# Attention and two feed-forward layers on one core: GpSimd's normalising in two multiplications, coefficients later, a plan that looks ahead

## The chip, the core and the metric

The kernel runs on one core of a Trainium2 chip. The core has five engines that run side by side, each through its own list of instructions in order: TensorE (PE in the tables, with its weight loads as PEld), VectorE (DVE), ScalarE (ACT), GpSimd (POOL) and SyncE (SP), which here only issues transfers. They meet at semaphores. The metric is the device time of one execution in microseconds, the median of the runs shown; less is better.

## What is computed

Two batches of 12 heads, 448 tokens, head dimension 64, causal attention in float32; its output, laid out as 896 tokens by 768, goes through two feed-forward layers of 768 by 2048 by 768. The first has the gate `h * clip(h+3, 0, 6) / 6`, the second a rational function of `h` with six coefficients `a` and `b`:

```
attn = softmax(mask(q @ k.T / 8)) @ v          # per head; x = attn as (896, 768)
h = x @ w_in;  x = (h * clip(h + 3, 0, 6) / 6) @ w_out
h = x @ w_in2
P = a[0] + a[1]*h + a[2]*h**2 + a[3]*h**3
Q = 1 + |b[0]|*|h| + |b[1]|*h**2
out = (P / (Q + 1e-6)) @ w_out2
```

The weights arrive as float64; the kernel takes their two halves apart and builds from each a rounded float32 part and a rest, and every product of the feed-forward layers is the sum of three products (high by high, high by rest, rest by high).

## The kernel before, and what sets its order

**Attention** works on 12 pairs of heads, numbered 0 to 11. Queries are cut into seven pieces of 64, and piece `r` (0 to 6) sees 64(r+1) keys; two heads lie side by side on the 128 partitions. For each pair:

- SP loads keys, queries and values (`kr`, `qr`, `v`; L401, L406, L407).
- PE multiplies the scores into four PSUM banks (L434, 28 products).
- VectorE adds the mask, takes each row's maximum and copies the piece to SBUF as `e<r><x>`, where x is the pair's parity (L446). So there are two sets of `e` buffers, and pair n+2 can enter them only when pair n has left.
- ScalarE takes the exponential in place and sums it (L453, an activation and a read of its accumulator).
- The sums get 1e-9 added (L463 on ScalarE or L465 on VectorE) and are inverted on VectorE (L469), in two parts: pieces 6, 5, 0 first, then 4, 3, 2, 1. This is in `stat`.
- The pieces are normalised, that is multiplied by the inverse, on ScalarE (L475), VectorE or GpSimd (both L477). Before the change GpSimd does the three widest pieces, r = 6, 5 and 4, of the pairs 1 to 9, and the others do the rest.
- PE transposes the normalised pieces in four groups of four (L483), VectorE or ScalarE moves each group to SBUF as `et` (L335, L333), and PE multiplies by the values (L503). ScalarE and VectorE split the result into `xh` and `xl`.

**The products** (L722) start when the attention of most pairs is done: 128 chunks of three weight tiles, 2304 products of 128 by 128 by 448, of which 18 belong to a chunk. For each chunk ScalarE and VectorE build the weights out of the raw bits: `full` (L617), `tail` (L623), shift and sign (L627, L633), the high part `w` (L333) and the rest (L651). A ring of four `w` buffers lets them run ahead of PE. Every third product chunk from the second layer on is prepared early, stored to DRAM (`kept`) and fetched later. The coefficients `ca` and `cb` (L593, L594) are needed only by the rational function in the second half; VectorE makes `cneg` of them (L597) and ScalarE `cabs` (L600).

**The order** is not written by hand. `add` gives each operation a kind, a time at which it is wanted, the engines it can run on with a price for each, and what it reads and writes. `order` then plays a list scheduler: at each step it takes, of all operations whose inputs are planned, the one that can begin first, and of several with the same beginning the one that is due first (`DUE` by kind, added to its wanted time). `STAY` is a handicap for a change of PE's tiling. The chosen order is what each engine's list of instructions gets; on the chip only the order counts, not the planned times.

Of the kernel before, what the change touches and what calls it, by code (L numbers as in the profile page):

```python
# [35 lines left out]
class Program:  # L36
# [15 lines left out]

    TILING = {"scores": "quarters", "apply": "columns"}
    DRAIN = 0.16
    STAY = 2.84

    def __init__(self, rings, banks, due):
        self.rings, self.banks, self.due = rings, banks, due
# [2 lines left out]
    def add(self, kind, at, engines, fn, *args, reads=(), writes=(), new=()):  # L61

        self.ops.append((kind, at, engines, fn, args, tuple(reads), tuple(writes), tuple(new)))

    def order(self):
# [42 lines left out]
        due = [op[1] + self.due[op[0]] for op in ops]  # L110
        result, tiling = [], ""
        while can:
            best = None
            for n, t in can.items():
                room, want = 0.0, {}
                for tag, key in ops[n][7]:
                    want[tag] = want.get(tag, 0) + 1
                    if tag == "w" and key != queue[-1]:
                        room = 1e9
                for tag, k in want.items():  # L120
                    if tag in self.rings:
                        keys, size = rings[tag], self.rings[tag]
                        for back in range(size - k + 1, size + 1):
                            if len(keys) >= back:
                                room = max(room, released.get(keys[-back], 1e9))
                    else:
                        times = sorted(x for x in banks if x is not None)
                        if live[tag] + k > self.banks[tag] or len(times) < k:
                            room = 1e9
                        else:  # L130
                            room = max(room, times[k - 1])
                if room >= 1e9:
                    continue
                turn = "pe" in t and self.TILING.get(ops[n][0], "") != tiling
                for e, cost in ops[n][2].items():
                    mine = max(t[e], free[e], room), due[n] + self.STAY * turn, n, e, cost
                    if best is None or mine < best:
                        best = mine
            if best is None:
                raise RuntimeError("no room")  # L140
            begin, _, n, e, cost = best
            if e == "pe" and self.TILING.get(ops[n][0], "") != tiling:
                tiling = self.TILING.get(ops[n][0], "")
                begin = max(begin, free[e] + self.DRAIN)
            start[n], end[n], where[n] = begin, begin + cost, e
            free[e] = end[n]
            del can[n]
            got = []
            for tag, key in ops[n][7]:
                if tag == "w":  # L150
                    queue.pop()
                if tag in self.rings:
                    rings[tag].append(key)
                else:
                    b = min((x, b) for b, x in enumerate(banks) if x is not None)[1]
                    banks[b] = None
                    held[key] = tag, b
                    live[tag] += 1
                    got.append(b)
            given[n] = got  # L160
            for key in {*ops[n][5], *ops[n][6]}:
                touch[key] -= 1
                last[key] = max(last.get(key, 0.0), end[n] + self.DELAY[e]["dve"])
                if not touch[key]:
                    released[key] = last[key]
                    if key in held:
                        tag, b = held.pop(key)
                        banks[b] = last[key]
                        live[tag] -= 1
            for u in users[n]:  # L170
                missing[u] -= 1
                if not missing[u]:
                    can[u] = earliest(u)
            result.append((begin, len(result), n))
# [9 lines left out]
def c_act(n):  # L184
    return 0.051 + n / 1200
# [8 lines left out]


def c_norm(n, r, w):
    fast = {"dve": 0.07 + w / 960, "act": 0.06 + w / 1200}
    if 0 < n < 10 and r > 3:
        return {"pool": 0.25 + w * 0.00252}
    return fast if n == 0 or r > 3 else {**fast, "pool": 0.25 + w * 0.00252}  # L200


def c_pe(n, passes):
# [7 lines left out]
def c_mm(n, passes):  # L211
# [2 lines left out]


DUE = {
    "load": -66.8,
    "keep": 0.0,
    "fetch": -20.0,
    "load v": -6.2,  # L220
    "norm": -71.7,
    "scores": 73.4,
    "max": -32.0,
    "exp": 10.8,
    "bias": 4.9,
    "reciprocal": -29.8,
    "transpose": -21.5,
    "move": 6.5,
    "apply": 23.1,
    "x hi": 5.2,  # L230
    "x rest": 62.2,
    "constants": -8.8,
    "w load": -87.2,
    "magnitude": 45.8,
    "tail": -50.0,
    "shift": -31.3,
    "sign": -2.7,
    "w hi": 63.9,
    "w rest": -7.0,
    "product": 0.0,  # L240
    "relu": 8.8,
    "gate": 1.1,
    "g hi": -5.5,
    "g rest": 21.7,
    "y hi": 20.8,
    "y rest": 12.6,
    "affine": 7.8,
    "times": -0.9,
    "abs": 6.2,
    "times2": -4.8,  # L250
    "slope": -0.4,
    "square": -3.2,
    "ln": 21.9,
    "exp2": -3.5,
    "over": 16.5,
    "newton": 17.1,
    "value": -6.1,
    "r hi": 19.2,
    "r rest": 3.2,
    "out": -3.6,  # L260
    "store": 7.5,
}
PAIR = 5.6

# [19 lines left out]
def tile_attention_moe_moe2(  # L284
# [36 lines left out]
        "p": 4, "qy": 3,  # L321
    }
    rings.update({f"e{r}": EB for r in range(NCH)})
    prog = Program(rings, {"s": 4, "t": 2, "o": 2, "sum": 8}, DUE)
    add = prog.add
    bank = [psum.tile([P, 512], F32, name=f"bank{n}") for n in range(prog.BANKS)]

# [143 lines left out]
    def a_norm(e, n, r):  # L471
        t, at_ = es[n % EB][r][:, :(r + 1) * CP], LINEUP.index(r)
        by = tiles["stat", n][:, 2, at_:at_ + 1]
        if e is nc.scalar:
            e.activation(t, t, AF.Copy, scale=by)  # L475
        else:
            e.tensor_scalar(t, t, by, None, ALU.mult)  # L477

    def a_transpose(e, n, g, banks):
        pt = tiles["pt", n, g] = bank[banks[0]]  # L480
# [39 lines left out]
    for n in range(len(pairs)):  # L520
# [59 lines left out]
                new=[("o", ("o", n))] if a == 0 else (),  # L580
            )
        b, hp = pairs[n]
        add("x hi", t, {"act": c_act(S) + 0.04}, a_hi, n, reads=[("o", n)], writes=[("x", hp, b)])
        add("x rest", t, {"dve": c_dve(S)}, a_lo, n, reads=[("o", n)], writes=[("x", hp, b)])


# [11 lines left out]

    def c_abs(e):
        e.activation(cabs, cb, AF.Abs)  # L600

    add("constants", 20, {"dma": 0.1}, c_load, writes=["c"])
    add("constants", 30, {"dve": 0.1}, c_neg, reads=["c"], writes=["cneg"])
    add("constants", 30, {"act": 0.1}, c_abs, reads=["c"], writes=["cabs"])


    raw, full, tail, split = {}, {}, {}, {}
# [57 lines left out]
    def add_chunk(i, t, early=()):  # L665
# [12 lines left out]
        add("shift", t, dve, w_shift, i, reads=[("tail", i)], writes=[("full", i)])  # L678
        add("sign", t, dve, w_sign, i, reads=[("raw", i)], writes=[("full", i)])
        x = [("x", hp, b) for hp in range(KM) for b in range(B)] if early and i == early[0] else []  # L680
        add(
            "w hi", t, act, w_hi, i, bool(early), reads=[("full", i)] + x, writes=[key],
            new=[(tag, key)],
# [194 lines left out]
    for n, c in enumerate(early):  # L878
        add_chunk(c, base + 40 + (whole - 45) * n / len(early), early)
    while i < len(chunks):  # L880

        side = chunks[i][0][0] == 2
        n = 1 if not side else 2 if chunks[i + 2][0][0] == 2 else 3
# [72 lines left out]
```

## Time and profile before

| | us |
|---|---|
| median of 3 runs | 552.57 (552.07 to 553.94) |
| the profiled execution, whole | 552.57 |
| its span, first to last instruction | 550.8 |
| PE busy in the span | 537.6 (98%) |
| VectorE, ScalarE, GpSimd busy | 429.5, 404.0, 39.6 |

The profiled execution has the median's time, and 1.77 us of it lie outside the span. The span falls into two stages. Up to about 95 us the core does attention, with the first 48 products mixed in; from there to 547.3 us PE runs products, and 3.5 us of copy and store close it. A busy engine need not be the bound in a stage: what tells is who waited for whom. In the rows, times count from the start of the span; an entry in square brackets is the idle time of an engine just before the row and what ended it. On PE a busy time includes waiting that falls within a run of merged instructions, so the time from one row's start to the next row's start is the better measure.

### The profile page before, as it was taken

How to read it: one execution, taken by the hardware profiler on the slowest of the kernel's cores; microseconds unless marked ns; L12 is line 12 of the kernel's file. 1: busy time of each engine (PE TensorE's matmuls, PEld its weight loads, DVE VectorE, ACT ScalarE, POOL GpSimd, SP SyncE). 2: the span in 40 equal slices, each digit the busy share in tenths (PEclk: the TensorE clock that was granted, in tenths of full speed). 3: DMA queues.
4: the chain of work that ended last, by engine and by line, in shares of the span. 5: the costliest groups of instructions: out<-in, count | busy, mean ns of one | idle time of the engine just before them, and what ended most of it. 6: DMA issues, size and time to landing. Idle time of an engine off the chain costs nothing.

```text
span 550.8 us, 9402 instructions
## 1 busy us (share of the span) xinstructions
PE 537.6 (98%) x3236; PEld 491.7 (89%) x3236; DVE 429.5 (78%) x953; ACT 404.0 (73%) x907; POOL 39.6 (7%) x51
## 2 busy tenths in 40 slices
PE   6889999999999999999999999999999999999997
PEld 5667788999999999999999999999999999999996
DVE  3769896799999997877776279999899988975420
ACT  4989997888888987767676269877787678755410
POOL 2555531000000000000000000000000000000000
PEclk9899999999999999999999999999999999999999
DMA  5764224267777878677776431154234324236100
GB/s 168 217 190 136 64 65 137 68 225 249 229 251 237 270 229 295 224 265 249 249 245 202 135 115 58 59 174 141 87 115 125 105 87 134 96 114 200 50 35 33
DMA packets 39312, 87.13 MB, mean 158 GB/s; under 512 B 4704, under 2 KB 14688, under 8 KB 39264
## 3 DMA queue, kind: packets, MB, share of 16 engines
q1 hardware_dynamic: 39104, 86.30, 49.1%
q8 instruction: 25, 0.41, 0.3%
q10 hardware_dynamic: 160, 0.23, 0.2%
q14 instruction: 23, 0.19, 0.1%
HBM read 71.18 MB, written 15.34 MB: 157 GB/s over the span
## 4 chain that ended last, share of the span: by engine, by line
PE 90%; ACT 6%; SPq 1%; DMA 1%; issue 1%; POOL 1%; DVE 0%; POOLq 0%; ACTq 0%
PE bank L722 84%; ACT e L453 3%; PE bank L503 2%; PE bank L483 2%; PE bank L434 2%; DMA cb<-in_b 1%; PE bank L383 1%; ACT e L475 1%; ACT et L333 1%; POOL e L477 0%; SPq L401 0%; ACT xh L333 0%; SPq L407 0%; SPq L406 0%; ACT full L617 0%
## 5 line engine op out<-in xcount | busy, mean ns | idle before, releaser
L722 PE MATMUL bank<-yh,w 128*128 128x448 f32 x384 | 112.1, 362 | 0.0
L722 PE MATMUL bank<-rh,w 128*128 128x448 f32 x384 | 97.2, 362 | 0.0
L722 PE MATMUL bank<-xh,w 128*128 128x448 f32 x384 | 94.0, 364 | 0.0
L722 PE MATMUL bank<-ph,w 128*128 128x448 f32 x384 | 92.6, 362 | 0.0
L651 DVE TENSOR_TENSOR w<-full,w 128x384 fp32r<-128x384 f32 x96 | 53.1, 555 | 47.2 <-ACT w L333 47.0
L333 ACT ACTIVATE w<-full 128x384 fp32r<-128x384 f32 x96 | 50.4, 528 | 53.2 <-PE bank L722 52.7
L623 ACT ACTIVATE tail<-raw 128x384 uint32<-128x384 uint8 x128 | 69.7, 557 | 20.9 <-DVE full L627 18.1
L617 ACT ACTIVATE full<-raw 128x384 f32<-128x384 f32 x128 | 68.9, 554 | 15.9 <-DVE w L651 15.0
L627 DVE SCALAR_TENSOR_TENSOR full<-full,tail 128x384 uint32<-128x384 uint32 x128 | 69.6, 555 | 12.7 <-ACT full L617 11.3
L722 PEld LDWEIGHTS bank<-rh,w 128*128 128x128 f32 x384 | 71.7, 187 | 5.6 <-DMA w<-kept 0.6
L722 PEld LDWEIGHTS bank<-ph,w 128*128 128x128 f32 x384 | 72.0, 188 | 4.9
L722 PEld LDWEIGHTS bank<-xh,w 128*128 128x128 f32 x384 | 71.6, 188 | 5.3 <-DVE stat L469 0.4
L722 PEld LDWEIGHTS bank<-yh,w 128*128 128x128 f32 x384 | 72.0, 187 | 4.7
L633 DVE SCALAR_TENSOR_TENSOR full<-raw,full 128x384 uint32<-128x384 uint32 x128 | 69.0, 554 | 1.6
L722 PE MATMUL bank<-yl,w 128*128 128x448 f32 x192 | 69.5, 362 | 0.0
L722 PE MATMUL bank<-rl,w 128*128 128x448 f32 x192 | 54.6, 362 | 0.0
L722 PE MATMUL bank<-xl,w 128*128 128x448 f32 x192 | 53.9, 362 | 0.0
L722 PE MATMUL bank<-pl,w 128*128 128x448 f32 x192 | 53.9, 362 | 0.0
L453 ACT ACTIVATE e<-e,stat 128x192 f32<-128x192 f32 (+6 forms) x84 | 42.4, 522 | 6.6 <-DVE stat L446 6.6
L477 POOL TENSOR_SCALAR e<-e,stat 128x448 f32<-128x448 f32 (+4 forms) x31 | 36.9, 1201 | 47.1 <-DVE stat L469 42.3
L446 DVE CUSTOM_DVE_ANT_0 e<-bank,mask 128x192 f32<-128x192 f32 (+6 forms) x84 | 31.8, 415 | 8.8 <-PE bank L434 8.6
L722 PEld LDWEIGHTS bank<-yl,w 128*128 128x128 f32 x192 | 36.0, 188 | 2.5
(58 smaller groups left out, 739.2 us busy)
## 6 DMA issues: line engine op xcount, KB each, us to landing
raw<-in_w SPq DMA_DIRECT2D x128, 384.0 KB, 3.6
kept<-ws SPq DMA_DIRECT2D x32, 384.0 KB, 4.2
w<-kept SPq DMA_DIRECT2D x32, 384.0 KB, 3.4
kr<-in_kT SPq DMA_DIRECT2D x24, 112.0 KB, 2.8
out_T<-o SPq DMA_DIRECT2D x12, 224.0 KB, 2.8
qr<-in_qT SPq DMA_DIRECT2D x22, 112.0 KB, 3.1
v<-in_v SPq DMA_DIRECT2D x12, 128.0 KB, 3.1
v<-in_v SPq DMA_DIRECT2D x12, 96.0 KB, 2.8
```

The lines of the kernel that those rows point to most:

```text
L333: e.activation(out, in_, AF.Copy)
L434: e.matmul(tiles["sc", n, r][halves[slot]], q[halves[j], r * CP:w], k[halves[j], :w], start=True, stop=True,)
L446: e.tensor_tensor_reduce(es[n % EB][r][:, :w], tiles.pop(("sc", n, r)), mask[:, S - w:], -0.125, 3.0e38, ALU.add, ALU.min, tiles["stat", n ...
L453: e.activation(t, t, AF.Exp, bias=stat[:, 0, at_:at_ + 1], scale=-1.0, accum_out=stat[:, 1, at_:at_ + 1],)
L477: e.tensor_scalar(t, t, by, None, ALU.mult)
L483: e.transpose(to[:, x], es[n % EB][r][:, c * P:(c + 1) * P], ident)
L617: e.activation(full[i], high, AF.Copy, scale=TO_F32)
L623: e.activation(tail[i], top, AF.Copy, bias=-31.0 / 64.0, scale=1.0 / 32.0)
L627: e.scalar_tensor_tensor(bits, bits, 3, tail.pop(i), ALU.logical_shift_left, ALU.bitwise_or)
L633: e.scalar_tensor_tensor(bits, raw.pop(i)[:, :, :, 1], 0x80000000, bits, ALU.bitwise_and, ALU.bitwise_or)
L651: e.tensor_tensor(split[i][:, 1], full.pop(i), split[i][:, 0], ALU.subtract)
L722: e.matmul(sums[which, m, b], split[i][:, w, j, :], x, start=k == 0 and n == 0, stop=last and n == 2,)
```

## The change

Five things are changed together.

1. Normalising on VectorE and GpSimd becomes one `tensor_scalar` with two multiplications, by the inverse and then by 1.0, in place of one multiplication and no second operation. The result is the same.
2. All seven pieces of the pairs 1 to 9 are now normalised on GpSimd; only pairs 0, 10 and 11 have a choice of engines.
3. For the first four weight chunks the high part and the rest may be done on GpSimd too; the plan puts the high parts of chunks 0 to 3 there and the rests of chunks 0 and 2.
4. The coefficients are loaded among the products (after chunk 8's weights in the plan) and `cneg` and `cabs` made later still.
5. The planner looks ahead: up to 90 us of planned time, an operation that begins up to `LOOK` later than the earliest one on its engine counts as beginning equally early, and the one that is due first is taken. The due times of most kinds, `STAY`, the price of `x hi` and the number of banks for the values' product (2 to 1) change with it.

```diff
-    STAY = 2.84
+    STAY = 3.13
+    LOOK = {"pe": 0.153, "dve": 0.041, "act": 0.000, "pool": 1.171, "dma": 0.000}
+    UNTIL = 90.0
...
-                    mine = max(t[e], free[e], room), due[n] + self.STAY * turn, n, e, cost
-                    if best is None or mine < best:
-                        best = mine
+                    at = max(t[e], free[e], room)
+                    begins[e] = min(begins.get(e, at), at)
+                    found.append((at, due[n] + self.STAY * turn, n, e, cost))
...
+            begin, _, _, n, e, cost = min(
+                (max(at, begins[e] + self.LOOK[e] * (at < self.UNTIL)), late, at, n, e, cost)
+                for at, late, n, e, cost in found
+            )
...
 def c_norm(n, r, w):
-    fast = {"dve": 0.07 + w / 960, "act": 0.06 + w / 1200}
-    if 0 < n < 10 and r > 3:
-        return {"pool": 0.25 + w * 0.00252}
-    return fast if n == 0 or r > 3 else {**fast, "pool": 0.25 + w * 0.00252}
+    fast = {"dve": 0.13 + w / 1920, "act": 0.185 + w / 1200}
+    slow = {"pool": 0.12 + w * 0.0012}
+    return {**fast, **slow} if n == 0 or n > 9 else slow
...
-    "norm": -71.7,
-    "scores": 73.4,
+    "norm": -208.80,
+    "scores": 150.38,
...
-    prog = Program(rings, {"s": 4, "t": 2, "o": 2, "sum": 8}, DUE)
+    prog = Program(rings, {"s": 4, "t": 2, "o": 1, "sum": 8}, DUE)
...
-            e.tensor_scalar(t, t, by, None, ALU.mult)
+            e.tensor_scalar(t, t, by, 1.0, ALU.mult, ALU.mult)
...
-    add("constants", 20, {"dma": 0.1}, c_load, writes=["c"])
-    add("constants", 30, {"dve": 0.1}, c_neg, reads=["c"], writes=["cneg"])
-    add("constants", 30, {"act": 0.1}, c_abs, reads=["c"], writes=["cabs"])
...
+        act, dve = ({**e, "pool": c} if i < 4 else e for e, c in ((act, 0.5), (dve, 1.05)))
...
+        if i == 16:
+            add("constants", t, {"dma": 1.2}, c_load, reads=[("w", 8)], writes=["c"])
+        if i == 24:
+            add("constants", t, {"dve": 0.1}, c_neg, reads=["c", ("w", 20)], writes=["cneg"])
+            add("constants", t, {"act": 0.1}, c_abs, reads=["c", ("w", 20)], writes=["cabs"])
```

The tables say little by themselves; what follows is what the engines' lists show. The names are buffers: `e61` is piece 6 in the set of the odd pairs, `stat1` the statistics of pair 1, `et0_1` the second transposed group of pair 0, `bank2` a PSUM bank, `full0` the weights of chunk 0.

GpSimd, from the first normalising on (pairs 1 and 2), before:

```order
L477 TENSOR_SCALAR e61_104<-e61_104,stat1_214 128x448
L477 TENSOR_SCALAR e51_103<-e51_103,stat1_214 128x384
L477 TENSOR_SCALAR e41_102<-e41_102,stat1_214 128x320
L477 TENSOR_SCALAR e60_97<-e60_97,stat2_281 128x448
L477 TENSOR_SCALAR e50_96<-e50_96,stat2_281 128x384
```

and the same place in the changed kernel, where pair 1 has all seven pieces:

```order
L484 TENSOR_SCALAR e61_104<-e61_104,stat1_211 128x448
L484 TENSOR_SCALAR e51_103<-e51_103,stat1_211 128x384
L484 TENSOR_SCALAR e01_98<-e01_98,stat1_211 128x64
L484 TENSOR_SCALAR e41_102<-e41_102,stat1_211 128x320
L484 TENSOR_SCALAR e31_101<-e31_101,stat1_211 128x256
L484 TENSOR_SCALAR e21_100<-e21_100,stat1_211 128x192
L484 TENSOR_SCALAR e11_99<-e11_99,stat1_211 128x128
```

All seven pieces of a pair stand in a row where three stood, the part with the pieces 6, 5 and 0 first. Further on, between pairs 5 and 6, GpSimd's list in the changed kernel has the first weight chunk:

```order
L484 TENSOR_SCALAR e21_100<-e21_100,stat5_559 128x192
L484 TENSOR_SCALAR e11_99<-e11_99,stat5_559 128x128
L342 CAST w0_714<-full0_463 128x384
L654 TENSOR_TENSOR w0_714<-full0_463,w0_714 128x384
L484 TENSOR_SCALAR e60_97<-e60_97,stat6_656 128x448
```

The high part (CAST) and the rest (TENSOR_TENSOR) of chunk 0 have come to stand between two pairs; before, GpSimd had no weight work.

VectorE, around the first inverse of pair 1 (`stat1`, the RECIPROCAL of 3 columns; ISA is the mask and maximum of a piece), before:

```order
L335 COPY et0_2_291<-bank6_79 128x512
L446 ISA e00_91,stat2_281<-bank2_75,mask_90 128x64
L446 ISA stat2_281 128x1
L469 RECIPROCAL stat1_214<-stat1_214 128x3
L446 ISA e40_95,stat2_281<-bank4_77,mask_90 128x320
```

and in the changed kernel:

```order
L472 TENSOR_SCALAR stat1_211<-stat1_211 128x3
L453 ISA e00_91,stat2_281<-bank2_75,mask_90 128x64
L453 ISA stat2_281 128x1
L476 RECIPROCAL stat1_211<-stat1_211 128x3
L453 ISA e50_96,stat2_281<-bank5_78,mask_90 128x384
```

The copy of pair 0's third transposed group has gone from ahead of this inverse to a place behind it.

ScalarE, around the coefficients (`cabs`) in the middle of pair 4's exponentials, before:

```order
L453 ACTIVATE e20_93,stat4_455<-e20_93,stat4_455 128x192
L453 ACTIVATE e30_94,stat4_455<-e30_94,stat4_455 128x256
L600 ACTIVATE cabs_111<-cb_109 128x2
L453 ACTIVATE e10_92,stat4_455<-e10_92,stat4_455 128x128
L617 ACTIVATE full0_563<-raw0_250 128x384
L453 ACTIVATE e61_104,stat5_561<-e61_104,stat5_561 128x448
L475 ACTIVATE e30_94<-e30_94,stat4_455 128x256
L475 ACTIVATE e10_92<-e10_92,stat4_455 128x128
```

and in the changed kernel:

```order
L460 ACTIVATE e20_93,stat4_461<-e20_93,stat4_461 128x192
L340 ACTIVATE xh1_84<-bank2_75 128x448
L460 ACTIVATE e50_96,stat4_461<-e50_96,stat4_461 128x384
L460 ACTIVATE e30_94,stat4_461<-e30_94,stat4_461 128x256
L460 ACTIVATE e10_92,stat4_461<-e10_92,stat4_461 128x128
L620 ACTIVATE full1_541<-raw1_274 128x384
L620 ACTIVATE full2_551<-raw2_291 128x384
L340 ACTIVATE et3_1_557<-bank5_78 128x512
L626 ACTIVATE tail0_565<-raw0_223 128x384
```

The coefficients and the normalising are gone from there, and weight work has come in.

## Rows read from the trace of the kernel before

**Rows 1.** Chain of work that ended last: start, us, engine, what, line, instructions.

```profile
8.56 3.16 ACT e L453 x12
...
42.42 0.48 ACT et L333
...
64.09 0.45 ACT tail L623
...
68.81 1.67 PE bank L434 x22
70.48 1.91 PE bank L503 x32
...
86.72 1.90 PE bank L483 x16
...
95.35 451.96 PE bank L722 x2256
```

**Rows 2.** Windows: stretch, us, busy PE, PEld, DVE, ACT, POOL, granted clock, DMA.

```profile
5.98:41.89 35.91, 29.19 (x356) 21.73 (x357) 26.14 (x122) 29.68 (x108) 14.84 (x12) 0.95 0.69 198
41.89:66.83 24.94, 23.34 (x294) 18.51 (x293) 21.55 (x84) 24.94 (x85) 15.05 (x12) 1.00 0.36 100
```

**Rows 3.** Timeline of PE: start, us, line, operands, count, [idle before, releaser].

```profile
5.91 3.98 PE L434 MATMUL bank<-kr,qr 64*64 64x64 f32 x56
12.69 1.37 PE L483 MATMUL bank<-ident,e 128*128 128x128 f32 x8 [2.81 <-DVE e L477]
13.99 3.07 PE L434 MATMUL bank<-kr,qr 64*64 64x64 f32 x28
...
18.32 1.75 PE L434 MATMUL bank<-kr,qr 64*64 64x64 f32 x28
21.70 1.97 PE L483 MATMUL bank<-ident,e 128*128 128x128 f32 x16 [1.64 <-POOL e L477]
...
37.92 0.33 PE L434 MATMUL bank<-kr,qr 64*64 64x64 f32 x4
...
41.89 2.16 PE L483 MATMUL bank<-ident,e 128*128 128x128 f32 x16
```

**Rows 4.** Timeline of VectorE, at pair 1's first inverse and at the coefficients.

```profile
15.83 0.62 DVE L446 CUSTOM_DVE_ANT_0 e<-bank,mask 128x448 f32<-128x448 f32 x1 [0.68 <-PE bank L434]
...
17.99 0.69 DVE L335 COPY et<-bank 128x512 f32<-128x512 f32 x1 [1.53 <-PE bank L483]
...
37.28 0.17 DVE L597 TENSOR_SCALAR cneg<-ca 128x4 f32<-128x4 f32 x1 [2.24 <-DMA ca<-in_a]
```

**Rows 5.** Timeline of ScalarE, the coefficients.

```profile
38.16 0.20 ACT L600 ACTIVATE cabs<-cb 128x2 f32<-128x2 f32 x1 [2.60 <-DMA cb<-in_b]
```

**Rows 6.** Timeline of GpSimd: normalising, three widths in a row, then single ones.

```profile
19.01 3.70 POOL L477 TENSOR_SCALAR e<-e,stat 128x448 f32<-128x448 f32 x3 [15.48 <-DVE stat L469]
...
61.16 3.69 POOL L477 TENSOR_SCALAR e<-e,stat 128x448 f32<-128x448 f32 x3 [1.19 <-DVE stat L469]
...
77.90 1.05 POOL L477 TENSOR_SCALAR e<-e,stat 128x256 f32<-128x256 f32 x1 [1.13 <-DVE stat L446]
84.89 0.45 POOL L477 TENSOR_SCALAR e<-e,stat 128x64 f32<-128x64 f32 x1 [5.95 <-DVE stat L469]
```

**Rows 7.** Groups by line: GpSimd's other operations that read and write SBUF (busy, mean ns); two weight groups.

```profile
L368 POOL TENSOR_SCALAR_AFFINE_SELECT mask<-mask 64x64 f32<-64x64 f32 x2 | 0.5, 236 | 0.1
masks.py:199 POOL TENSOR_SCALAR_AFFINE_SELECT ident<-ident 128x128 f32<-128x128 f32 x1 | 0.3, 295 | 0.1
...
L333 ACT ACTIVATE w<-full 128x384 fp32r<-128x384 f32 x96 | 50.4, 528 | 53.2 <-PE bank L722 52.7
...
L627 DVE SCALAR_TENSOR_TENSOR full<-full,tail 128x384 uint32<-128x384 uint32 x128 | 69.6, 555 | 12.7 <-ACT full L617 11.3
```

**Rows 8.** Timeline of VectorE beside a GpSimd operation that ran from 61.16 on.

```profile
62.05 0.54 DVE L465 TENSOR_SCALAR stat<-stat 128x4 f32<-128x4 f32 x1 [0.79 <-ACT e L453]
...
62.95 0.58 DVE L627 SCALAR_TENSOR_TENSOR full<-full,tail 128x384 uint32<-128x384 uint32 x1
```

More of the change, by code (lines that the diff above doesn't have):

```diff
@@ L112, in order @@
         while can:
-            best = None
+            found, begins = [], {}
             for n, t in can.items():
@@ L135, in order @@
                 for e, cost in ops[n][2].items():
-                    mine = max(t[e], free[e], room), due[n] + self.STAY * turn, n, e, cost
-                    if best is None or mine < best:
-                        best = mine
-            if best is None:
+                    at = max(t[e], free[e], room)
+                    begins[e] = min(begins.get(e, at), at)
+                    found.append((at, due[n] + self.STAY * turn, n, e, cost))
+            if not found:
                 raise RuntimeError("no room")
-            begin, _, n, e, cost = best
+            begin, _, _, n, e, cost = min(
+                (max(at, begins[e] + self.LOOK[e] * (at < self.UNTIL)), late, at, n, e, cost)
+                for at, late, n, e, cost in found
+            )
+            begin = next(at for at, _, m, x, _ in found if m == n and x == e)
             if e == "pe" and self.TILING.get(ops[n][0], "") != tiling:
@@ L216 @@
 DUE = {
[L217 to L220, printed above, removed]
-    "norm": -71.7,
-    "scores": 73.4,
[L223 to L261, printed above, removed]
+    "load": 6.72,
+    "keep": 0.00,
+    "fetch": -20.00,
+    "load v": -48.90,
+    "norm": -208.80,
+    "scores": 150.38,
+    "max": -32.47,
+    "exp": -3.18,
+    "bias": -83.75,
+    "reciprocal": -25.17,
+    "transpose": -138.70,
+    "move": 9.04,
+    "apply": -49.35,
+    "x hi": -72.35,
+    "x rest": 155.41,
+    "constants": -2.74,
+    "w load": -49.96,
+    "magnitude": 100.54,
+    "tail": 111.81,
+    "shift": 113.26,
+    "sign": -36.25,
+    "w hi": 136.49,
+    "w rest": 4.62,
+    "product": 0.00,
+    "relu": -84.58,
+    "gate": 6.85,
+    "g hi": -36.16,
+    "g rest": 172.87,
+    "y hi": 20.80,
+    "y rest": 12.60,
+    "affine": 7.80,
+    "times": -0.90,
+    "abs": 6.20,
+    "times2": -4.80,
+    "slope": -0.40,
+    "square": -3.20,
+    "ln": 21.90,
+    "exp2": -3.50,
+    "over": 16.50,
+    "newton": 17.10,
+    "value": -6.10,
+    "r hi": 19.20,
+    "r rest": 3.20,
+    "out": -3.60,
+    "store": 7.50,
 }
@@ L582, in tile_attention_moe_moe2 @@
         b, hp = pairs[n]
-        add("x hi", t, {"act": c_act(S) + 0.04}, a_hi, n, reads=[("o", n)], writes=[("x", hp, b)])
+        add("x hi", t, {"act": c_act(S)}, a_hi, n, reads=[("o", n)], writes=[("x", hp, b)])
         add("x rest", t, {"dve": c_dve(S)}, a_lo, n, reads=[("o", n)], writes=[("x", hp, b)])
```

## The prediction

> **What bounds the kernel now.** I read the chain of waits first, then busy time by stretch, then PE's timeline before 95 us, then the timelines of the engines that PE waits for there. The chain [rows 1] ends in 451.96 us of products without a gap: 2256 products at 0.2003 us. Nothing shortens these, so the change can win only before 95.35 us, in attention. PE's own prices there, from the same chain, are per pair of heads 1.67 us for scores, 1.90 for transposes and 1.91 for the values' product, together 5.48. Twelve pairs are 65.8 us, and the 48 products mixed in 9.6: 75.4 us of work. PE starts it at 5.91 and finishes at 95.35, which is 89.4 us. So 14.0 us is waste, and no version with this work can win more.
>
> Where the waste lies follows from the starts of PE's rows [rows 2, 3], each stretch less its work at these prices. (a) 5.91 to 18.32: 12.4 us for three scores and one pair's transposes (6.9): 5.5 wasted in filling the pipeline. It holds a wait of 2.81 for the first normalised pieces and a score of 3.07 for 1.67, with a granted clock of 0.95 over the larger stretch. (b) 18.32 to 41.89: 23.6 us for four scores, three pairs' transposes, three values' products (18.1): 5.5 wasted. (c) 41.89 to 66.83: 24.9 us for three scores, five pairs' transposes, four values' products (22.2): 2.8 wasted. ScalarE is busy there for 24.94 us of 24.94: it sets the pace. (d) From 66.83 on: 0.3.
>
> **The change, part by part.** *The inverse of pair 1.* PE's wait of 1.64 us before 21.70 [rows 3] was for GpSimd, which began only at 19.01; the inverse stood on VectorE behind a copy of `et`, which itself waited 1.53 us for PE's transposes [rows 4]. The new list has that copy behind the inverse. The inverse then waits for the first maximum of pair 2, which began at 15.83 [rows 4], 1.84 after its scores; with these about 0.4 later (the fill, below) and the maximum's 0.62, GpSimd starts at about 17. Pieces 6 and 5 would be done before PE has finished the scores of pair 3 at 20.0, even at the old price (2.7 us for the two): the 1.64 goes. What is late next is the copies for the first values' product, done about 20.2; PE has a half pair of transposes before that. I take 1.6.
>
> *The coefficients.* ScalarE waits 2.60 us and VectorE 2.24 for them in the middle of attention [rows 4, 5]. Behind these waits stand exponentials, maxima and copies; the scores that PE begins at 37.92 need banks which VectorE empties, and take until 41.89, 3.97 us for 1.67. So 2.3 us of (b) is this wait, and it goes. The load now stands on SP among weight loads; behind it on VectorE and ScalarE is weight work that is ahead of PE, as the 52.7 us show in which ScalarE waits for PE to free a `w` buffer [rows 7]. I cost the move at nothing; without that cover it would be the same 2.6 us once.
>
> *Normalising.* ScalarE and VectorE lose it for pairs 1 to 9. For GpSimd three widths (1152 columns) take 3.7 us now, 256 columns 1.05, 64 columns 0.45 [rows 6]; with 192 and 128 between the last two (0.85 and 0.65), all seven cost 6.5 at one multiplication. What two cost no row shows. Low end: GpSimd's select, which also reads and writes each element, takes 236 ns for 64 columns and 295 for 128 [rows 7], so 0.92 ns a column and 0.18 fixed, 2.9 us a pair. High end: every column pays twice, 13 us. The nearest row in form is the single multiplication, 6.5. I take the low end all the same, because the select does more per column for a third of the price: the single multiplication's 3.2 ns a column is not what the engine needs to read, compute and write, but what the code behind this one form costs, and the second operation gives the instruction another form. That is the least certain step, but the forecast doesn't need all of it: up to about 4.9 us a pair GpSimd stays under PE's 5.48 with the weight work between (five operations, 0.5 to 1.3 each by the rows of GpSimd, about 0.5 a pair).
>
> The Trainium skill's "GPSIMD Engine Reference", § 3.1, says that a loop body with up to two operations per element is bound by its ports at 1.03 cycles per element at 1.2 GHz, so two should cost no more than one. For one multiplication the trace disagrees, 3.2 ns against 0.86; if two do reach it, a pair would cost about 2.8 with the select's fixed time, an estimate from that page, and the sum would not change.
>
> *The pace from pair 4 on.* Counting ScalarE's new list from the first exponential of pair 4 to that of pair 10: 42 exponentials (3.16 us for six of a pair, and about 0.4 for the seventh), 16 copies of `et` and `xh` at up to 0.48, 9 weight operations at 0.45, 6 small ones at 0.1 [rows 1]: 33.7 us, or 5.6 a pair at most, against PE's 5.48. The normalising is gone, but weight work has moved into its place. VectorE was busy 21.55 of 24.94 us in (c) [rows 2], lost its normalising and gained half a copy a pair. So PE, ScalarE and VectorE are nearly level, and of the 2.8 us in (c) I take 1.5 as won, between 0 and 2.8: six pairs at 0.1 lost to ScalarE, and about as much again to waits between engines that run level.
>
> *The rest of (b)*, 1.5 us in small waits, among them for GpSimd and for ScalarE's sums: I take 0.8 as won, between 0 and 1.5. *The fill (a)*: the first transposes still wait for the first exponentials, maximum and inverse; the bias before that inverse moves to VectorE and a piece of 384 to ScalarE. Three values' loads now stand ahead of pair 2's queries on SP, about 3.7 us of issue; these then land at about 13.4, just before the scores of pair 2 can start. I take 0, between -0.5 and +0.5.
>
> *After attention.* PE's products are the same and from chunk 3 on in the same order. Chunks 0 to 3 are ready earlier, chunks 5 and 6 have fewer gate operations ahead of them, and later ones stand as far ahead of PE as before. I take 0; a gap here would cost its own length.
>
> Sum: 1.6 + 2.3 + 1.5 + 0.8 = 6.2 us, of the 8.3 that (b) and (c) hold. The profiled execution took 552.57, its span 550.8 with 1.77 around it, and is the median of the runs shown. **552.57 - 6.2 = 546.4 us.**
>
> **The rivals.** *Level engines don't keep PE's pace.* The waste of (c) stays, 2.8, and half of the coefficients' 2.3 comes back as waits for ScalarE: won is 1.6 + 1.2 + 0.4 = 3.2, 549.4 us. For it speaks that ScalarE's list is at 5.6 a pair; against it, that ScalarE has 21 normalisings less in attention overall. One mechanism that belongs here is a lock between VectorE and GpSimd. A bias of four columns on VectorE took 0.54 us, where four columns of coefficients took 0.17, with GpSimd at work from 61.16 on [rows 4, 6, 8]; but a shift with two SBUF inputs took 0.58, hardly more than its mean of 0.555, with GpSimd at work beside it too [rows 7, 8]. If every shift and sign in pairs 4 to 9 did wait half a GpSimd operation, 0.3 us, seven would cost 2.1 us of VectorE's time and PE perhaps 1, giving 547.4. The Trainium skill's "SBUF — State Buffer", § Who interferes with whom, states that lock for both kinds; by the bias the trace agrees, by the shift it doesn't.
>
> *GpSimd's second multiplication is not cheaper (the change doesn't do what it says).* Then the end is on the other side. GpSimd becomes the bound of attention: from 17 on nine pairs at 6.5 (58.5) and five weight operations at up to 1.0 (5) end at 80.5. Behind that PE has four values' products (7.6), 40 transposes (4.8) and 30 products (6.0), so attention ends at 98.9. Before, it ended at 95.35 with 18 products (3.6) more done, so 91.7 by the same measure: 7.2 slower, 559.8 us. It turns from gain to loss at (91.7 - 18.4 - 5 - 17) / 9 = 5.7 us a pair, 88% of the price of one multiplication. With twice the price, 13 a pair, it is 58 us more, about 618. The row for the single multiplication speaks for it, the select against it.
>
> *Gaps among the products*: weight work that is due at other times starves PE somewhere after 95 us and eats the gain: about 552. Against it, ScalarE waits for PE there and not the other way.
>
> **How the numbers follow.** The forecast (544.2 to 547.5) has a chance of 0.58, the slower pace (547.5 to 550.5) 0.23, GpSimd at one multiplication's price or above 0.13, gaps that leave about nothing 0.06. The likeliest is the forecast, 546.4. The range goes from all of (b) and (c) won and a little of the fill, 8.3 + 0.3, so 544.0, to the end of the slower pace, 550.5: 0.81. A measurement of this kernel tells 0.3% from no change, 1.7 us, so between 550.9 and 554.2 counts as the same. Faster is forecast and slower pace, 0.81; the same 0.06; slower 0.13.
>
> **What would show it.** Right: a GpSimd row of 448 columns near 0.6 us and seven below 3.5; no wait of ScalarE or VectorE for the coefficients before the products; PE's wait for GpSimd near 20 us gone; values' products of pairs 3 to 7 some 5.6 us apart; the last gapless piece of the chain starting about 9 us earlier, near 85.5, and 18 products longer (3.6). Wrong: GpSimd rows of 448 columns at 1.4 us or more with PE waiting for them; a pace of 5.8 or more a pair with ScalarE busy throughout; a gap among the products.

## The result, and the profile after

| | before | after |
|---|---|---|
| median, us | 552.32 (551.7 to 553.94, 4 runs) | 545.87 (544.96 to 546.7, 4 runs) |
| profiled execution; its span | 552.57; 550.8 | 545.67; 543.9 |

The ratio is 0.9878, interval 0.9852 to 0.9905: 6.7 us faster by the ratio, 6.45 between the medians, where 6.2 were forecast.

**Attention.** The long pieces of the chain of waits of the changed kernel (start, us, what):

```profile
1.36 4.64 PE bank L390 x20
6.00 1.42 PE bank L441 x12
...
8.18 2.68 ACT e L460 x10
...
30.96 1.90 PE bank L490 x16
32.86 1.91 PE bank L510 x32
34.77 1.67 PE bank L441 x22
...
84.29 230.02 PE bank L726 x1149
...
365.51 174.93 PE bank L726 x873
```

PE's own prices are those of [rows 1] (scores 1.67, transposes 1.90, values 1.91), but from 13.70 to 59.91 every link of the chain is now PE itself, but for 0.04 us of issue. The stretch of products begins at 84.29, with 30 products done. Before, it began at 95.35 with 48 done [rows 1]; 18 fewer are 3.6 us, so 91.75 by the same measure. Attention ends 7.46 us earlier. Of that, 0.6 goes again among the products (below); 7.46 - 0.6 is the 6.9 us of the spans.

The windows (stretch, us, busy PE, PEld, DVE, ACT, POOL, granted clock, DMA share, GB/s) show whom PE no longer waits for:

```profile
5.90:18.30 12.40, 9.35 (x113) 6.79 (x116) 9.31 (x46) 9.48 (x36) 1.50 (x3) 0.86 0.67 185
18.30:41.90 23.60, 23.56 (x327) 18.73 (x319) 22.55 (x97) 23.21 (x81) 15.80 (x34) 1.00 0.74 217
41.90:66.80 24.90, 24.31 (x335) 20.10 (x332) 24.22 (x93) 23.80 (x84) 16.75 (x34) 1.00 0.45 137
```

In the last two PE is busy 47.87 of 48.50 us. In the second of [rows 2] it was ScalarE that had no idle time, 24.94 of 24.94; now it has 1.1 us. VectorE is as full. PE's timeline, with idle time and its releaser in brackets:

```profile
12.55 1.15 PE L490 MATMUL bank<-ident,e 128*128 128x128 f32 x8 [3.05 <-ACT e L482]
...
32.79 1.98 PE L510 MATMUL bank<-et,v 128*64 128x128 f32 x32
...
38.30 1.98 PE L510 MATMUL bank<-et,v 128*64 128x128 f32 x32
...
60.62 1.98 PE L510 MATMUL bank<-et,v 128*64 128x128 f32 x32 [0.29 <-DVE et L342]
...
66.04 1.98 PE L510 MATMUL bank<-et,v 128*64 128x128 f32 x32 [0.30 <-DVE xl L522]
```

The three with a bracket, and one of 1.4 at the very start, are all the waits that the profile lists for PE before 84 us. ScalarE's and VectorE's lists have none for the coefficients any more [rows 4, 5]. The wait for the first normalised pieces stayed (2.81 before, [rows 3]). By the prediction's own count, starts of rows less work at these prices, 5.0 us are wasted up to 17.85, 0.45 up to 41.89 and 0.8 up to 66.04, where it was 5.5, 5.5 and 2.8.

GpSimd's groups of the changed kernel up to 90 us (busy, mean ns of one, then idle) and two rows of its timeline, against [rows 6]:

```profile
L484 POOL TENSOR_SCALAR e<-e,stat 128x448 f32<-128x448 f32 x9 | 5.8, 643 | 24.3 <-DVE stat L476 13.7 <-PE bank L490 6.1 <-DVE stat L453 2.3
...
L484 POOL TENSOR_SCALAR e<-e,stat 128x64 f32<-128x64 f32 x10 | 3.4, 335 | 0.8 <-DVE stat L472 0.8
```

```profile
16.78 1.50 POOL L484 TENSOR_SCALAR e<-e,stat 128x448 f32<-128x448 f32 x3 [13.23 <-DVE stat L476]
...
21.55 3.21 POOL L484 TENSOR_SCALAR e<-e,stat 128x448 f32<-128x448 f32 x7 [0.47 <-DVE stat L453]
```

Seven pieces cost 3.2 us in this row and up to 3.6 in others, less than three did (3.7), and GpSimd starts at 16.78 instead of 19.01.

**Products.** One wait of PE after 84 us is in the list, on its timeline:

```profile
352.63 0.47 PE L726 MATMUL bank<-yh,w 128*128 128x448 f32 x1 [0.26 <-DVE p L778]
```

From 314.31 to 352.63 the chain leaves PE and runs mostly over VectorE's rational function. The 252 products from 314.31 to 365.51 took 51.2 us; at 0.2003 they are 50.5. So 0.7 is lost in this place, 0.26 of it as a visible wait; before, this stretch had no gap [rows 1].

### The profile page after: what moved, and what is told of

Its sections match the earlier page's. It is cut to its first block, busy times and chain, and to the rows that moved or that the text cites. A ratio compares the mean times of both kernels' runs of the same rounds, so it can differ in the third digit from the quotient of the medians.

```text
span 543.9 us, 9407 instructions
## 1 busy us (share of the span) xinstructions
PE 535.1 (98%) x3236; PEld 491.0 (90%) x3236; DVE 429.5 (79%) x946; ACT 394.2 (72%) x874; POOL 37.3 (7%) x91
## 4 chain that ended last, share of the span: by engine, by line
PE 90%; DVE 7%; ACT 1%; issue 1%; POOL 0%; POOLq 0%
PE bank L726 78%; PE bank L490 4%; PE bank L510 4%; PE bank L441 3%; PE bank L390 1%; DVE p L775 1%; DVE p L778 1%; DVE qy L799 1%; DVE qy L791 1%; DVE p L803 1%; DVE p L801 1%; DVE rl L785 1%; DVE e L453 1%; ACT e L460 1%; DVE et L342 0%
## 5 line engine op out<-in xcount | busy, mean ns | idle before, releaser
L340 ACT ACTIVATE w<-full 128x384 fp32r<-128x384 f32 x92 | 48.1, 523 | 48.4 <-PE bank L726 48.0
L630 DVE SCALAR_TENSOR_TENSOR full<-full,tail 128x384 uint32<-128x384 uint32 x128 | 70.7, 562 | 13.7 <-ACT full L620 12.0
L460 ACT ACTIVATE e<-e,stat 128x320 f32<-128x320 f32 (+6 forms) x84 | 41.5, 496 | 7.6 <-DVE stat L453 7.4
L453 DVE CUSTOM_DVE_ANT_0 e<-bank,mask 128x384 f32<-128x384 f32 (+6 forms) x84 | 31.7, 414 | 9.3 <-PE bank L441 8.3
L726 PEld LDWEIGHTS bank<-rl,w 128*128 128x128 f32 x192 | 36.0, 187 | 2.6
```

The costliest lines, as they stand in the source:

```text
L340: e.activation(out, in_, AF.Copy)
L453: e.tensor_tensor_reduce(es[n % EB][r][:, :w], tiles.pop(("sc", n, r)), mask[:, S - w:], -0.125, 3.0e38, ALU.add, ALU.min, tiles["stat", n ...
L460: e.activation(t, t, AF.Exp, bias=stat[:, 0, at_:at_ + 1], scale=-1.0, accum_out=stat[:, 1, at_:at_ + 1],)
L630: e.scalar_tensor_tensor(bits, bits, 3, tail.pop(i), ALU.logical_shift_left, ALU.bitwise_or)
L726: e.matmul(sums[which, m, b], split[i][:, w, j, :], x, start=k == 0 and n == 0, stop=last and n == 2,)
```

## The experiments

In the table the end of attention is the start of the long stretch of products in the profiled run, reduced to 30 products done (0.2 us for each beyond or short of that). Each ratio is to runs of the kernel before taken beside that run (medians 551.92 to 552.37). Line numbers move by a few with the edits.

| run | kernel | median, us | ratio to before, interval | attention ends |
|---|---|---|---|---|
| | before | | | 91.75 |
| e1_one_mult | after, one multiplication | 564.15 | 1.0214 (1.0195 to 1.0233) | 102.55 |
| e2_two_mult | before, two multiplications | 552.68 | 1.0013 (1.0002 to 1.0024) | 92.4 |
| e3_coef_late | before, coefficients late | 549.72 | 0.9957 (0.994 to 0.9973) | 89.05 |
| e4_inverse | before, inverse of pair 1 early | 552.21 | 1.0004 (0.9993 to 1.0015) | 92.1 |
| e5_three | e2, e3, e4 together | 549.49 | 0.9954 (0.9938 to 0.997) | 89.46 |
| e6_three_v | e5, values' loads early | 549.64 | 0.9958 (0.9945 to 0.9971) | 89.0 |
| e7_pool | e2, all normalising of pairs 1 to 9 on GpSimd | 549.58 | 0.9959 (0.9943 to 0.9975) | 88.16 |
| e8_pool_all | e6 and e7 together | 545.54 | 0.9886 (0.9869 to 0.9903) | 84.83 |
| e9_scalar_norm | after, two pieces a pair back on ScalarE | 548.88 | 0.9938 (0.9921 to 0.9955) | 86.5 |
| e10_values_late | after, values' loads late | 552.12 | 0.9996 (0.9984 to 1.0008) | 91.1 |
| e11_no_look | after, no look-ahead | 550.93 | 0.9978 (0.9965 to 0.9991) | 89.8 |
| e12_pool_coef | e3 and e7 together | 546.70 | 0.9895 (0.9881 to 0.991) | 85.76 |
| | after | 545.87 | 0.9878 (0.9852 to 0.9905) | 84.29 |

**e1: one multiplication in the changed kernel.**

```diff
-            e.tensor_scalar(t, t, by, 1.0, ALU.mult, ALU.mult)
+            e.tensor_scalar(t, t, by, None, ALU.mult)
```

> The changed kernel, its order untouched, with one multiplication in place of two on every engine that normalises. Theory (the second multiplication makes GpSimd's normalising cheap, and the new order depends on it): GpSimd needs 6.5 us a pair by the rows of the kernel before, nine pairs 58.5, and with 3.5 of weight work (0.50 and 1.01 an operation in the trace of the changed kernel) from 16.8 on it ends near 79; with 18.4 us of PE work behind that attention ends near 97 with 30 products done, 13 us later than 84.2: about 559 us, GpSimd rows of 448 columns at 1.4 us. Rival (order and coefficients bring the gain, the form of the operation matters little): under 549 us.

Measured 564.15, 18.3 us above the changed kernel. Its GpSimd groups up to 110 us:

```profile
L484 POOL TENSOR_SCALAR e<-e,stat 128x448 f32<-128x448 f32 x9 | 12.7, 1407 | 14.9 <-DVE stat L476 13.4 <-DVE stat L472 1.5
...
L484 POOL TENSOR_SCALAR e<-e,stat 128x64 f32<-128x64 f32 x10 | 4.9, 486 | 0.0
```

Same place, same work, 1407 ns against 643. PE waits 10.5 us for GpSimd in eight waits. So the rest of the change depends on the second multiplication: without it that rest makes the kernel 2.1% slower, and by more than expected (below). By itself the second multiplication gives nothing (e2, next).

**e2 to e4: one part each in the kernel before.** The reorderings of e3 and later change the finished list of operations. Here and below, a line that begins with # stands for code that is left out:

```diff
-        for (_, _, _, fn, args, _, _, _), e, banks in self.order():
+        todo = self.order()
+        # e3: c_load goes ahead of weight load 14, c_neg and c_abs ahead of weight load 22
+        # e4: move (0, 2) goes behind reciprocal (1, 0)
+        for (_, _, _, fn, args, _, _, _), e, banks in todo:
```

> The kernel before, order untouched, with the two multiplications alone. GpSimd's three widths should take 1.5 us in place of 3.7. Theory (each part does its own share): PE's waits for GpSimd, 1.64 and two of 0.4, go, ScalarE still sets the pace in the middle: 550 to 551.5 us. Rival (cheap normalising is the whole gain): about 546.

> The kernel before, its order untouched but for the coefficients' load, which goes behind the load of chunk 13's weights, and the two operations made of them, which go ahead of the load of chunk 22's. Theory (the 2.3 us that the scores of pair 6 lose are this wait): 2.3 us less, about 550.2 us, the scores that took 3.97 us take 1.7 to 2.2. Rival (ScalarE's pace behind it takes most back, since it is busy throughout afterwards): under 0.8 us, 551.7 or more.

> The kernel before, its order untouched but for one copy on VectorE (third transposed group of pair 0), which goes behind the first inverse of pair 1. Theory: GpSimd's first normalising starts near 17.4 in place of 19.0 and PE's wait of 1.64 us before 21.7 goes: about 550.9 us. Rival (another input of the transposes, or the values' product behind them, is late next): the wait shrinks by less than half or comes back behind it, 552.

The coefficients alone gave 2.4 us (552.3 times 0.0043; 2.7 in the traces), the prediction's 2.3. The other two gave nothing, against what was expected; for e4 its rival came true. In e4 GpSimd did start earlier, at 16.73, and PE's wait for it fell from 1.64 to 1.10, but PE's timeline then shows:

```profile
23.92 2.97 PE L508 MATMUL bank<-et,v 128*64 128x128 f32 x32 [2.54 <-DMA v<-in_v]
```

The first product with the values waits 2.54 us for the values themselves. In the order before, SP issues them only at 19.60. In e2 the same wait stands at 23.96 (1.52) and 30.52 (1.44).

**e5 and e6: the parts together, then with the values.** e6 moves three loads ahead of pair 2's keys:

```diff
+        # loads of values 0 to 2 go ahead of load ("kr", 2)
```

> The kernel before, engines and order untouched but for three things together: two multiplications, coefficients late, the one copy behind the first inverse of pair 1. Theory S (ScalarE's own list is the bound from 8.6 us to the end of attention; it stood idle there only 1.05 and 2.60 us): as the coefficients alone, 549.3 to 549.9 us. Theory V (the early gains are there, and the values' loads, for which PE waited 1.5 to 2.5 us in the two runs before, take them): the same here, 549.7. Rival (the shares add up, as in the sum of the prediction): 547.5.

> As the run with the three things, and the loads of the values of pairs 0 to 2 ahead of pair 2's keys, as in the changed kernel. Theory S: still 549.0 to 549.7 us, since ScalarE has no less to do. Theory V: PE's waits for values go and 547 to 547.7 us.

Both stay at e3's time. The values were a wait behind the inverse, but not the bound: with that wait gone nothing came. The windows of e6 show what is left:

```profile
8.60:41.90 33.30, 28.86 (x334) 20.88 (x328) 27.25 (x121) 31.62 (x115) 8.42 (x14) 0.95 0.68 200
41.90:66.80 24.90, 23.70 (x324) 18.93 (x322) 21.57 (x90) 24.90 (x84) 6.12 (x11) 1.00 0.38 108
```

ScalarE (the fourth busy time) is idle 1.7 us of 58.2, and in e3's trace it was idle 1.6 us there already. Its list, 21 normalisings longer than in the changed kernel, is full from its first exponential on, and a wait removed elsewhere only ends in a wait for ScalarE.

**e7, e8, e12: normalising off ScalarE, in the old order.**

```diff
+        todo = [(op, "pool" if op[0] == "norm" and 0 < op[4][0] < 10 else e, banks) for op, e, banks in todo]
```

> The kernel before, order untouched, two multiplications, and every normalising of pairs 1 to 9 that ScalarE and VectorE did runs on GpSimd at the same place of the order; coefficients and values' loads stay. Theory S: ScalarE loses 21 normalisings of 0.33 us, 7 us, so the middle becomes free: 547.5 to 549.5 us, with PE then waiting for values and coefficients. Theory V: the loads cap it, 551 or more.

> All of these together in the order of the kernel before: normalising of pairs 1 to 9 on GpSimd by two multiplications, coefficients late, the one copy behind the inverse, values' loads early. Theory S, and V: 545.5 to 547 us, as the changed kernel, without its planner. Rival (the look-ahead and the new due times are what brings the gain): 548.5 or more.

> The kernel before in its old order with two multiplications, all normalising of pairs 1 to 9 on GpSimd, and the coefficients behind weight piece 13; pair 1's copy ahead of its inverse and the values' loads stay where they were. The first two gave 549.58 us together without the coefficients, and 545.54 us with coefficients, inverse and earlier values. Theory S with independent terms: the coefficients' 2.3 us come off, 547.0 to 547.6 us, and the other 1.7 us belong to pair 1's inverse and the values' loads. Rival (with ScalarE relieved the coefficients are the one wait left): 545.3 to 546.2 us. Second rival (the waits for values, 0.9 us, and pair 1's inverse hide the coefficients' gain): 548.5 us or more.

The edit takes 20 normalisings off ScalarE and 16 off VectorE. e7 alone gives 2.3 us, just above its theory's range in time; ScalarE still waits for the coefficients in it (2.98). With the coefficients moved as well (e12) it is 5.8, so the normalising is worth 3.3 beside them (89.05 to 85.76). That this is more than in e7 is not shown: the intervals allow the two gains to add up, and in e7's profiled execution, the quickest of its runs, attention ends 3.6 earlier than before. 546.70 lies between what the theory and its first rival expected. PE's timeline of e12 shows the values again:

```profile
22.86 1.98 PE L514 MATMUL bank<-et,v 128*64 128x128 f32 x32 [0.48 <-DMA v<-in_v]
...
28.84 1.98 PE L514 MATMUL bank<-et,v 128*64 128x128 f32 x32 [0.87 <-DMA v<-in_v]
```

e8, with early values and the inverse, has neither wait, and its attention ends 0.9 earlier; the intervals of e8 and e12 overlap, so that last step rests on the traces alone. e8 has the time of the changed kernel with the old planner: new due times, look-ahead and weight work on GpSimd bring nothing measurable beyond these five edits.

**e9: two pieces a pair back on ScalarE.** The edit takes pieces r = 1 and 2, which are 128 and 192 columns wide; the widths that its expectation names are wrong, the price is that of these two.

```diff
+        todo = [(op, "act" if op[0] == "norm" and 0 < op[4][0] < 10 and op[4][1] in (1, 2) else e, banks) for op, e, banks in todo]
```

> The changed kernel in its own order, except that the second and third pieces (384 and 320 wide) of pairs 1 to 9 are normalised by ScalarE, at the same place of the order, instead of GpSimd. Theory S (ScalarE's own list is what bounds the attention): each of the nine pairs puts two more normalisings on ScalarE, some 0.7 us a pair, 6 us in all, onto a list that was busy 23.21 of 23.60 us (18.3 to 41.9) and 23.80 of 24.90 us (41.9 to 66.8); the 0.4 and 1.1 us idle there take up some 1.5, and what is then left over in front of ScalarE's copies (about 1) a little more, so the last gapless piece of the products begins 3 to 5 us later: 549 to 551 us. Rival (TensorE's own 5.5 us a pair is the bound and ScalarE has slack): within 1 us of the changed kernel, 545.5 to 546.9.

Measured 548.88, just under the range expected and 3 us above the changed kernel; the attention ends 2.2 later. Windows of e9:

```profile
18.30:41.90 23.60, 21.92 (x296) 17.52 (x296) 20.52 (x86) 23.60 (x84) 11.89 (x24) 1.00 0.75 208
41.90:66.80 24.90, 23.92 (x327) 19.01 (x320) 22.62 (x88) 24.90 (x88) 13.07 (x25) 1.00 0.44 128
```

ScalarE is busy to the last hundredth again and PE loses 2.0 us to it. e9 moves work of ScalarE alone, where e12 freed VectorE too; from both sides, e12 against e3 and e9 against the changed kernel, normalising on ScalarE costs 2 to 3 us.

**e10: values late in the changed kernel.** Their loads go behind a weight piece and the keys and queries of a seventh load, so that SP issues the first of them at 21.19 us (4.55 in the changed kernel).

```diff
+        # weight load 3, loads ("kr", 6) and ("qr", 6), then values 0 to 2, go ahead of apply 0
```

> The changed kernel in its own order, except that the loads of the values of pairs 0 to 2 are queued on SyncE behind a weight piece and the queries and keys of a seventh load. Theory: the early loads of values are a condition of the gain, since in the old order with the attention made faster TensorE's products with the values waited for their load (1.4 to 2.5 us, a pair): here the first such product then waits some 2 to 2.7 us, and since TensorE is busy 23.56 of 23.60 us behind it, nothing gives it back: 547.5 to 548.5 us. Rival (in the new order the engines catch up): 545.5 to 546.3 us.

Measured 552.12: the whole gain is gone. PE's timeline and a window:

```profile
25.78 3.68 PE L516 MATMUL bank<-et,v 128*64 128x128 f32 x32 [5.44 <-DMA v<-in_v]
```

```profile
18.30:41.90 23.60, 18.16 (x228) 14.80 (x224) 15.35 (x69) 16.48 (x59) 11.44 (x26) 0.86 0.59 165
```

The loads came later than I had reckoned: in the chain the landing of a weight piece (6.58 us) stands ahead of them. The wait was 5.44, and the 32 products behind it took 3.68 instead of 1.98. The granted clock was 0.86 over the whole stretch, where the changed kernel has 1.00, and 0.50 over these products, which is the lower of its two levels (1.2 and 2.4 GHz); in the 5.58 us ahead of them PE was busy for 0.14:

```profile
20.20:25.78 5.58, 0.14 (x2) 0.03 (x1) 2.23 (x12) 2.79 (x11) 3.78 (x9) 0.74 0.75 202
25.78:29.46 3.68, 3.68 (x33) 3.12 (x34) 0.00 (x0) 0.00 (x0) 0.00 (x0) 0.50 0.17 48
```

Wait and slower products are together 7.1, of which attention lost 6.8. Next to nothing gave it back; but this place is 1.6 us later than in the kernel before (19.60), so it prices a late load, not this part of the change.

**e11: the planner without look-ahead.**

```diff
-    LOOK = {"pe": 0.153, "dve": 0.041, "act": 0.000, "pool": 1.171, "dma": 0.000}
+    LOOK = {"pe": 0.0, "dve": 0.0, "act": 0.0, "pool": 0.0, "dma": 0.0}
```

> The changed kernel with the planner's look-ahead at zero on all engines, so that the list is planned by the new costs and due times alone. Theory: the cause of the gain is that the normalising left ScalarE and that the coefficients' load moved; the look-ahead orders the same work a little better: 546 to 548 us. Rival (the look-ahead carries the order, since the due times were found with it): 549 us or more.

My theory fell: 550.93. With the new due times but no look-ahead the plan loads the values ahead of an early pair's queries. SP's timeline, then PE's:

```profile
3.27 0.64 SPq L413 DMA_DIRECT2D v<-in_v  x1
...
7.25 1.25 SPq L408 DMA_DIRECT2D qr<-in_qT  x2
```

```profile
10.24 2.42 PE L441 MATMUL bank<-kr,qr 64*64 64x64 f32 x28 [2.99 <-DMA qr<-in_qT]
```

In the changed kernel these queries are issued at 3.27, ahead of the values. At its first product with the values PE is 3.1 us behind the changed kernel (23.69 against 20.55); the other 2.4 by which attention ends later were not followed up. The look-ahead is needed where the due times were set for it; by e8 it is not a source of gain of its own.

## Why the prediction was right, and where it was not

**The total and its place were right.** (b) and (c) held 8.3 us of waste; 7.05 of it went, where 6.2 were forecast. The fill gave 0.5 (forecast 0, bound +0.5), and the products took 0.6 back (forecast 0). Its signs held but for two: the stretch of products starts at 84.29, not near 85.5, and is broken once; and of GpSimd's seven unbroken rows of seven pieces two are not below 3.5 (3.51 and 3.62). The lower end of the forecast, 544.2, should be the 544.0 of its own sum.

**GpSimd's price, the least certain step, was nearly right.** 2.9 us a pair was taken from the select's rows; 3.2 to 3.6 were measured, under the 4.9 up to which the forecast stood. The select gave the better price than the same operation with one multiplication, though the latter was nearer in form.

**The rival of one multiplication's price was real, but cheaper than the truth.** Forecast 559.8, measured 564.15 in e1. GpSimd's and PE's timelines of e1, where pair 9 leaves GpSimd:

```profile
75.15 6.90 POOL L484 TENSOR_SCALAR e<-e,stat 128x448 f32<-128x448 f32 x7
```

```profile
82.11 0.66 PE L490 MATMUL bank<-ident,e 128*128 128x128 f32 x4 [2.80 <-POOL e L484]
82.70 3.11 PE L510 MATMUL bank<-et,v 128*64 128x128 f32 x32
```

GpSimd is done with the nine pairs at 82.05 (80.5 counted, at 6.5 a pair). The prediction's own rows add up to 6.7 a pair, not 6.5 (3.7, 1.05, 0.85, 0.65 and 0.45), and e1's groups to 6.66. PE needs 20.5 us behind that (18.4 counted at full speed; the first product with the values alone took 3.11 instead of 1.98). That is the 3.6 us by which attention ended later than the rival had it.

**Coefficients, 2.3: right.** e3 measured 2.4 alone. The wait is in ScalarE's own list, the one that was full.

**Inverse of pair 1, 1.6: wrong as a term of its own.** It gave nothing alone (e4) and nothing beside the coefficients (e5 against e3). The step that failed is "what is late next": the prediction named the copies for the first product with the values, done about 20.2, and the values themselves were late, issued at 19.60. The loads that the new order puts early appeared in the prediction only as a risk to pair 2's queries. Even with them early (e6) nothing came, with ScalarE's list full but for 1.7 us.

**The pace, 1.5, and the rest of (b), 0.8: mis-sized and too narrow in place.** Normalising off ScalarE and VectorE gave 3.3 (e12 against e3) for the 2.3 of the two terms. The prediction saw ScalarE as the pace only in (c), from its 24.94 of 24.94; e6 shows its list full from the first exponential on, but for 1.7 us. So the gain that the prediction shared out by waits in (b) was mostly ScalarE's there too. Its count of ScalarE's new list, 5.6 a pair "at most", held as an upper bound: from pair 1 to pair 6 values' products stand 5.48 to 5.52 us apart (5.51 from 32.79 to 38.30), against PE's own 5.48, and from pair 6 to pair 7 5.84.

So the sum came out because the terms covered the same waste, not because each was right, and that 6.2 lies so near the measured 6.7 is in part luck: normalising gave more than its terms, and the inverse's 1.6 did not come. One after the other in the old order, by the traces: coefficients 2.7, normalising on GpSimd 3.3, inverse and values together 0.9; 6.9.

**The rivals.** Level engines did keep PE's pace (PE busy 47.87 of 48.50). The lock between VectorE and GpSimd has a trace. Of the changed kernel's first eight shifts on VectorE four began while GpSimd was at work; they are shown with one bias, and below them two GpSimd operations that ran beside the last two rows:

```profile
34.52 0.70 DVE L630 SCALAR_TENSOR_TENSOR full<-full,tail 128x384 uint32<-128x384 uint32 x1
...
40.04 0.68 DVE L630 SCALAR_TENSOR_TENSOR full<-full,tail 128x384 uint32<-128x384 uint32 x1
...
56.51 0.69 DVE L630 SCALAR_TENSOR_TENSOR full<-full,tail 128x384 uint32<-128x384 uint32 x1
...
58.94 1.03 DVE L630 SCALAR_TENSOR_TENSOR full<-full,tail 128x384 uint32<-128x384 uint32 x1
...
64.71 0.75 DVE L472 TENSOR_SCALAR stat<-stat 128x3 f32<-128x3 f32 x1
```

```profile
58.54 1.01 POOL L654 TENSOR_TENSOR w<-full,w 128x384 fp32r<-128x384 f32 x1
...
64.94 0.50 POOL L342 CAST w<-full 128x384 fp32r<-128x384 f32 x1
```

The shift's group from 100 to 300 us, where GpSimd is idle, and its line in e1 from 16 to 82 us (ns, least, median and most):

```profile
L630 DVE SCALAR_TENSOR_TENSOR full<-full,tail 128x384 uint32<-128x384 uint32 x87 | 47.3, 555 | 5.1 <-ACT full L620 4.7
```

```profile
L630 DVE SCALAR_TENSOR_TENSOR full<-full,tail x4: 545/554/572, 40.3 to 73.2; 128x384 uint32<-128x384 uint32 x4
```

Three of the four took some 0.14 us longer than the mean of 0.555 without GpSimd, and the one that began in the middle of GpSimd's TENSOR_TENSOR 0.47. Two biases took 0.48 (at 42.04) and 0.75 where others take 0.16. Together that is 1.8 us of VectorE's time, near the 2.1 of the rival; but PE's waits for VectorE sum to 0.6 (the bias at 64.71 stands in the chain ahead of the one at 66.04), where the rival gave PE 1. For shifts it goes by GpSimd's form, as far as these rows tell: in e1 all four began beside a single multiplication and took 0.55 to 0.57, as in [rows 8]. The Trainium skill's "SBUF — State Buffer", § Who interferes with whom, states an exclusive lock; the changed kernel's rows agree with it, the shifts of e1 don't. Gaps among the products did come, in one place and for 0.7 us, not the 6 of that rival.

**Open.** Whether the inverse or the values carry the last 0.9 between e12 and e8; how the 3.3 of e12 divide between ScalarE and VectorE (e9 has 2.2 in the traces for ScalarE alone, with 18 normalisings); why VectorE is later at 314 to 365 us in the new order (its 0.7 us are less than runs of this kernel can tell).

## What to carry to other kernels

When one engine's list is full, the waits that PE shows are not terms to be added up. Take the full list first: here what shortened it (the coefficients' wait, the normalising) gained by itself, while a wait removed elsewhere turned into a wait for that engine and gained nothing. For each wait that goes, look also at the loads of the next step, by the time at which they are issued. And price a new form of an instruction from another form that does as much per element, not from the old form's price.

## What the hardware showed that was not expected

GpSimd's multiplication by a scalar costs a third per column with a second multiplication by 1.0: (643 - 335) / 384 = 0.80 ns a column against (1407 - 486) / 384 = 2.40 in the same place of the same order. The Trainium skill's "GPSIMD Engine Reference", § 3.1, gives one price for bodies with up to two operations, 1.03 cycles an element, by estimate 0.86 ns at the page's 1.2 GHz. The form with two comes out near it and a little below, the form with one does not; why one is dearer no run here shows. And a wait of PE can cost more than itself: in e10 the 32 products behind a wait of 5.44 us took 1.7 longer, at a granted clock of 0.50.
